# The clamp and the last subtraction of a float64 weight conversion, moved from VectorE to GpSimd

## The chip, the core and the metric

The kernel runs on one core of one Trainium2 chip. The core has TensorE (matmuls; PE in the profile, its weight loads PEld), VectorE (DVE), ScalarE (ACT) and GpSimd (POOL), and SyncE (SP), whose queue issues the DMAs of this kernel. The metric is the device time of one execution in microseconds (us); smaller is better.

## What is computed

Eight batches of an attention with a packed query, and then a feed-forward layer over all tokens:

```python
def sm_attn(qq, kk, vv):
    s = scale * np.matmul(qq, kk.transpose(0, 1, 3, 2))
    s = s - np.max(s, axis=-1, keepdims=True)
    a = np.exp(s)
    a = a / (np.sum(a, axis=-1, keepdims=True) + 1e-09)
    return np.matmul(a, vv)
p_packed = sm_attn(p, k, v)
out = sm_attn(q, p_packed, p_packed)
...
h = x @ w_in
g = np.maximum(h, 0.0) + alpha * np.minimum(h, 0.0)
return (g @ w_out).astype(np.float32)
```

There are 8 batches, 8 heads, 576 tokens, 64 columns per head and 32 packed queries; w_in is 512 x 2048 and w_out 2048 x 512. The activations are float32. The two weight matrices arrive as float64, and the kernel takes them as pairs of 32-bit words.

## The kernel before

Heads are taken in pairs (4 pairs, 128 partitions). `attention(b, tp)` does half a batch: it loads k, v and q, splits a float32 operand into a high part in the rounded format of the matmul and a low part that is the rest (`split_x`, L176; `split_v`, L306), and multiplies with both. The splits' low parts are GpSimd subtractions (L180, L311). For batches from 1 on, GpSimd also does the subtraction and the multiplication of the second softmax (L432, L439) and the low part of the result (L456). Batches 0 and 1 (`exact=True`) run on float32 without splits of q, k and v.

`packed_w` and its relatives multiply the packed values with w_in; `first(k, f)` gives one of 16 blocks f of the hidden layer for half a batch k (288 tokens), applies the leaky activation (L646 on ScalarE, L647 on VectorE) and splits the result (L652, L653); `second(k, f)` multiplies with block f of w_out and collects in four PSUM banks (L670 to L672).

**The conversion.** `convert` (L106) turns one tile of 128 x 512 float64 weights into float32. SP loads the raw words (L115). ScalarE takes the absolute value of the upper words, read as float32, into `mag` (L121), and the shifted lower words into `low` (L123). VectorE clamps `mag` to a range (L125), shifts its bits left by 3 and masks them (L128), puts sign and top bits from the raw tile in (L132), and adds `low` as an integer (L137 or L139). Where the whole float32 is wanted that is all (L137). Otherwise ScalarE rounds to the high part (L141), and VectorE subtracts it, which leaves the low part (L142). Every step reads what the step before it left in the same tile `mag`.

The conversion runs 32 times, every one with a clamp: 4 tiles of `packed_w_fine` and 4 of `packed_w_first` as whole float32; 8 tiles of `packed_w(..., "fresh")` and 16 of `convert_w_out` with high and low part, so that there are 24 subtractions. Eight more tiles of `packed_w(..., "whole")` are split by L573 and L574 without a conversion. The split w_in tiles are written to DRAM (L579) and read again by all later batches, so that conversions take place in the first quarter of the run only.

**What sets the order.** Each engine works through its own queue in order. The code is made of generators that the loop at L772 advances by a plan with start times (L759 to L769), around the sequence of `first` and `second`. This gives each instruction its place in the program; a planner with its own estimate of durations then fixes the order on each engine before the launch, and steps of several conversions and attentions are interleaved there much finer than the code reads. `mag` and `low` come from rings of three buffers (tags `xh` and `xl`, shared with `split_x`); the raw tiles from buffers that w_out tiles use later (`new_raw`, L144). A raw buffer can be loaded again when its last reader (L132) is through. All DMAs of the kernel stand in SP's single queue.

Of the kernel before, what the change touches and what calls it, by code (L numbers as in the profile page):

```python
# [13 lines left out]
ALU = mybir.AluOpType  # L14
# [8 lines left out]
def fv(ap):  # L23

    return ap.bitcast(F32)
# [3 lines left out]
def pack_attention_ffn_kernel(  # L29
# [20 lines left out]
    nc = tc.nc  # L50
# [24 lines left out]
    op = ctx.enter_context(tc.tile_pool(name="op", bufs=4))  # L75
# [30 lines left out]
    def convert(src, raw, place, whole=None, room=None):  # L106

        nc.sync.dma_start(out=raw if room is None else room, in_=src)  # L115
        yield
        u = raw.bitcast(U32).rearrange("p (f t) -> p f t", t=2)
        up = raw.bitcast(F32).rearrange("p (f t) -> p f t", t=2)[:, :, 1]
        mag = xin.tile([P, 512], F32, name="mag", tag="xh")
        bits = mag.bitcast(U32)  # L120
        nc.scalar.activation(out=mag, in_=up, func=AF.Abs)  # L121
        low = xin.tile([P, 512], U32, name="low", tag="xl")
        nc.scalar.activation(out=low, in_=u[:, :, 0], func=AF.Copy, scale=2.0**-29)  # L123
        yield
        nc.vector.tensor_scalar(  # L125
            out=mag, in0=mag, scalar1=F64_BOTTOM, scalar2=F64_TOP, op0=ALU.max, op1=ALU.min
        )
        nc.vector.tensor_scalar(  # L128
            out=bits, in0=bits, scalar1=3, scalar2=0x3FFFFFF8,
            op0=ALU.logical_shift_left, op1=ALU.bitwise_and,  # L130
        )
        nc.vector.scalar_tensor_tensor(  # L132
            out=bits, in0=u[:, :, 1], scalar=0xC0000000, in1=bits,
            op0=ALU.bitwise_and, op1=ALU.bitwise_or,
        )
        if whole is not None:
            nc.vector.tensor_tensor(out=whole().bitcast(U32), in0=bits, in1=low, op=ALU.add)  # L137
            return
        nc.vector.tensor_tensor(out=bits, in0=bits, in1=low, op=ALU.add)  # L139
        hi, lo = place()  # L140
        nc.scalar.copy(out=hi, in_=mag)  # L141
        nc.vector.tensor_tensor(out=lo, in0=mag, in1=fv(hi), op=ALU.subtract)  # L142

    def new_raw(f=0):  # L144

# [13 lines left out]
    def convert_w_out(f):  # L159
        def place():  # L160
            wo_t[f] = const.tile([P, 2, DM], F32R, name=f"wo{f}", tag=f"wo{f}")
            return wo_t[f][:, 0, :], wo_t[f][:, 1, :]

        return convert(w_out[f * P : (f + 1) * P, :], new_raw(f), place)
# [329 lines left out]
    def convert_w_in(j, pr, place, whole=None):  # L494
        src = w_in[pr * P : (pr + 1) * P, j * 512 : (j + 1) * 512]
        return convert(src, new_raw(), place, whole)

    def packed_w_fine(j):


        def get(f):
            cols = slice((4 * j + f) * P, (4 * j + f) * P + P)
            w = new_w32()
            raw = new_raw()
            steps = convert(
                w_in.rearrange("(r p) c -> p r c", p=P)[:, :, cols],
                raw, None, lambda: w, raw.rearrange("p (r c) -> p r c", r=NP),
            )
            drain(steps)
            nc.sync.dma_start(  # L510
                out=w_whole[j].rearrange("r p c -> p r c")[:, :, f * P : f * P + P],
                in_=w.rearrange("p (r c) -> p r c", r=NP),
            )
            return w
# [216 lines left out]
    def zipped(*gens):  # L731
# [11 lines left out]
        out=nal, in0=al, scalar1=-1.0, scalar2=1.0, op0=ALU.mult, op1=ALU.add  # L743
# [73 lines left out]
```

## Time and profile before

| | us |
|---|---|
| runs of the kernel before | 811.73, 815.4, 815.91 (median 815.4) |
| span of the profiled execution, first to last instruction | 809.3 |
| PE busy in the span | 773.0 |
| VectorE busy | 605.8 |
| ScalarE busy | 497.1 |
| GpSimd busy | 191.4 |
| clamps (L125) on VectorE, 32 | 13.3 |
| subtractions (L142) on VectorE, 16 + 8 | 10.9 + 5.7 |
| first and last clamp start | 13.0 and 202.1 |

The profile gives the span of its execution and no device time of its own beside it. The span leaves out what lies before the first and after the last instruction; the runs stand 2.4 to 6.6 us above it. Durations of VectorE instructions overlap by their pipeline, so that the distance of two starts is shorter than a duration. The rows of the profile have the form: line, engine, operation, output<-inputs, shapes, count, busy us and mean ns of one, idle time before it and what ended that. Timeline rows begin with start and length in us.

### The profile page before, as it was taken

How to read it: one execution, taken by the hardware profiler on the slowest of the kernel's cores; microseconds unless marked ns; L12 is line 12 of the kernel's file. 1: busy time of each engine (PE TensorE's matmuls, PEld its weight loads, DVE VectorE, ACT ScalarE, POOL GpSimd, SP SyncE). 2: the span in 40 equal slices, each digit the busy share in tenths (PEclk: the TensorE clock that was granted, in tenths of full speed). 3: DMA queues.
4: the chain of work that ended last, by engine and by line, in shares of the span. 5: the costliest groups of instructions: out<-in, count | busy, mean ns of one | idle time of the engine just before them, and what ended most of it. 6: DMA issues, size and time to landing. Idle time of an engine off the chain costs nothing.

```text
span 809.3 us, 14930 instructions
## 1 busy us (share of the span) xinstructions
PE 773.0 (96%) x5376; PEld 729.5 (90%) x5376; DVE 605.8 (75%) x1301; ACT 497.1 (61%) x1165; POOL 191.4 (24%) x195
## 2 busy tenths in 40 slices
PE   6779899999989899999999999999999999999997
PEld 4557688989989799999999999999999999999997
DVE  3998989877887656898896477987875566666664
ACT  4888798876767775665657756665567533333332
POOL 2101411235346212354342014534410000000000
PEclk9979999999999999999999999999999999999999
DMA  9976787422223843322216722311027000000000
GB/s 312 340 233 223 262 304 236 151 54 83 78 88 101 267 151 104 93 59 82 70 59 212 235 59 59 91 58 45 2 92 256 20 31 1 31 1 31 1 30 30
DMA packets 58457, 93.77 MB, mean 116 GB/s; under 512 B 5136, under 2 KB 36880, under 8 KB 58384
## 3 DMA queue, kind: packets, MB, share of 16 engines
q1 hardware_dynamic: 58384, 92.83, 35.7%
q8 instruction: 42, 0.69, 0.4%
q14 instruction: 31, 0.25, 0.1%
HBM read 72.88 MB, written 19.92 MB: 115 GB/s over the span
## 4 chain that ended last, share of the span: by engine, by line
PE 80%; DVE 8%; DMA 5%; ACT 5%; issue 1%; POOL 0%; SPq 0%; ACTq 0%; DVEq 0%
PE acc L670 15%; PE acc L671 15%; PE acc L672 15%; PE ps_h L640 7%; PE ps_h L641 7%; PE ps_h L642 7%; PE ps_h L628 3%; DMA vraw<-in_v 2%; PE ps_m L352 2%; PE ps_m L216 1%; PE ps_m L217 1%; PE ps_m L596 1%; PE ps_m L598 1%; PE ps_m L597 1%; DMA w<-w_split 1%
## 5 line engine op out<-in xcount | busy, mean ns | idle before, releaser
L670 PE MATMUL acc<-gh,wo 128*128 128x288 f32 x1024 | 286.2, 300 | 3.5 <-ACT gh L652 3.1
L671 PE MATMUL acc<-gh,wo 128*128 128x288 f32 x1024 | 281.8, 295 | 0.0
L670 PEld LDWEIGHTS acc<-gh,wo 128*128 128x128 f32 x1024 | 192.2, 188 | 9.8 <-ACT gh L652 5.6
L672 PE MATMUL acc<-gl,wo 128*128 128x288 f32 x1024 | 199.2, 299 | 0.0
L671 PEld LDWEIGHTS acc<-gh,wo 128*128 128x128 f32 x1024 | 192.4, 188 | 1.6 <-issue 0.2
L652 ACT CAST gh<-ps_h 128x288 fp32r<-128x288 f32 x256 | 101.6, 399 | 115.3 <-DVE ps_h L647 113.2
L646 ACT ACTIVATE neg<-ps_h 128x288 f32<-128x288 f32 x256 | 105.3, 412 | 107.2 <-PE ps_h L642 95.5
L653 DVE TENSOR_TENSOR gl<-ps_h,gh 128x288 fp32r<-128x288 f32 x256 | 115.2, 452 | 70.4 <-ACT gh L652 68.5
L647 DVE SCALAR_TENSOR_TENSOR ps_h<-neg,nal,ps_h 128x288 f32<-128x288 f32 x256 | 131.2, 515 | 47.2 <-ACT neg L646 46.5
L672 PEld LDWEIGHTS acc<-gl,wo 128*128 128x128 f32 x1024 | 157.4, 188 | 3.1 <-issue 0.4
L640 PE MATMUL ps_h<-a_h,pwh 128*128 128x288 f32 x448 | 134.2, 300 | 4.1 <-DVE gl L653 4.0
L641 PE MATMUL ps_h<-a_l,pwh 128*128 128x288 f32 x448 | 132.3, 295 | 0.0
L642 PE MATMUL ps_h<-a_h,pwl 128*128 128x288 f32 x448 | 132.1, 295 | 0.0
L180 POOL TENSOR_TENSOR xl<-xraw,xh 128x576 fp32r<-128x576 f32 x48 | 71.4, 1488 | 175.2 <-ACT xh L179 171.1
L616 DVE TENSOR_TENSOR pwl<-pw,pwh 128x512 fp32r<-128x512 f32 x112 | 83.7, 748 | 9.1 <-ACT pwh L613 3.5
L640 PEld LDWEIGHTS ps_h<-a_h,pwh 128*128 128x128 f32 x448 | 84.2, 188 | 6.1 <-DVE gl L653 5.3
L641 PEld LDWEIGHTS ps_h<-a_l,pwh 128*128 128x128 f32 x448 | 84.3, 188 | 0.6
L642 PEld LDWEIGHTS ps_h<-a_h,pwl 128*128 128x128 f32 x448 | 84.1, 188 | 0.2
L601 ACT COPY pw<-ps_m 64x512 f32<-64x512 f32 x120 | 69.6, 580 | 15.2 <-PE ps_m L598 12.5
L615 DVE CAST pwh<-pw 128x512 fp32r<-128x512 f32 x96 | 52.0, 542 | 28.6 <-PE ps_h L641 27.8
L311 POOL TENSOR_TENSOR vs<-vraw,vs 128x640 fp32r<-128x640 f32 x24 | 40.4, 1682 | 51.3 <-ACT vs L310 50.3
L628 PE MATMUL ps_h<-a_f,pw 128*128 128x288 f32 x128 | 39.6, 433 | 3.8 <-DVE a_f L444 3.0
(127 smaller groups left out, 991.4 us busy)
## 6 DMA issues: line engine op xcount, KB each, us to landing
w<-w_split SPq DMA_DIRECT2D x48, 512.0 KB, 4.2
xraw<-in_kT SPq DMA_DIRECT2D x32, 288.0 KB, 2.9
xraw<-in_qT SPq DMA_DIRECT2D x32, 288.0 KB, 2.9
outT<-ot SPq DMA_DIRECT2D x64, 144.0 KB, 2.2
vraw<-in_v SPq DMA_DIRECT2D x32, 256.0 KB, 2.9
wraw<-in_w_in SPq DMA_DIRECT2D x16, 512.0 KB, 5.6
wraw<-in_w_out SPq DMA_DIRECT2D x16, 512.0 KB, 4.9
w_split<-w SPq DMA_DIRECT2D x16, 512.0 KB, 4.2
```

Source lines behind the costliest of these rows:

```text
L180: nc.gpsimd.tensor_tensor(out=xl, in0=raw, in1=fv(xh), op=ALU.subtract)
L616: nc.vector.tensor_tensor(out=tl, in0=src, in1=fv(th), op=ALU.subtract)
L640: nc.tensor.matmul(ps[:, :HS], th[:, i, fs], a_h[:, i, tok], start=hi, stop=False)
L641: nc.tensor.matmul(ps[:, :HS], th[:, i, fs], a_l[:, i, tok], start=False, stop=False)
L642: nc.tensor.matmul(ps[:, :HS], tl[:, i, fs], a_h[:, i, tok], start=False, stop=lo)
L646: nc.scalar.activation(out=neg, in_=x, func=AF.Relu, scale=-1.0)
L647: nc.vector.scalar_tensor_tensor(out=x, in0=neg, scalar=nal[:, f : f + 1], in1=x, op0=ALU.mult, op1=ALU.add)
L652: nc.scalar.copy(out=gh, in_=x)
L653: nc.vector.tensor_tensor(out=gl, in0=x, in1=fv(gh), op=ALU.subtract)
L670: nc.tensor.matmul(acc[o][:, :HS], wo_t[f][:, 0, os_], gh, start=begin, stop=False)
L671: nc.tensor.matmul(acc[o][:, :HS], wo_t[f][:, 1, os_], gh, start=False, stop=False)
L672: nc.tensor.matmul(acc[o][:, :HS], wo_t[f][:, 0, os_], gl, start=False, stop=end)
```

## The change

The clamp (L125) and the last subtraction (L142) are issued to GpSimd; operands, operations, tiles and their place in the program stay.

```diff
         nc.scalar.activation(out=low, in_=u[:, :, 0], func=AF.Copy, scale=2.0**-29)
         yield
-        nc.vector.tensor_scalar(
+        nc.gpsimd.tensor_scalar(
             out=mag, in0=mag, scalar1=F64_BOTTOM, scalar2=F64_TOP, op0=ALU.max, op1=ALU.min
         )
...
         hi, lo = place()
         nc.scalar.copy(out=hi, in_=mag)
-        nc.vector.tensor_tensor(out=lo, in0=mag, in1=fv(hi), op=ALU.subtract)
+        nc.gpsimd.tensor_tensor(out=lo, in0=mag, in1=fv(hi), op=ALU.subtract)
```

## The prediction

> **What bounds it now.** I read the page first: its span, the forty slices and the chain that ended last.
>
> ```profile
> span 809.3 us, 14930 instructions
> DVE  3998989877887656898896477987875566666664
> POOL 2101411235346212354342014534410000000000
> PE 80%; DVE 8%; DMA 5%; ACT 5%; issue 1%; POOL 0%; SPq 0%; ACTq 0%; DVEq 0%
> ```
>
> A slice is 20.2 us. The chain is 80% PE, yet VectorE's digits are 8 and 9 in slices 2 to 7 while GpSimd's are 1 to 4. The conversions lie there, so I asked for busy times by stretch. The columns are the stretch, its length, then busy time and count for PE, PEld, DVE, ACT and POOL, the clock, DMA share and GB/s.
>
> ```profile
> 20.00:66.00 46.00, 36.15 (x179) 25.74 (x179) 44.15 (x96) 36.07 (x87) 5.64 (x12) 0.89 0.86 284
> 66.00:93.00 27.00, 25.20 (x134) 18.14 (x132) 23.86 (x47) 21.62 (x52) 7.36 (x8) 1.00 0.73 245
> 93.00:107.00 14.00, 13.55 (x74) 10.22 (x75) 12.29 (x23) 12.59 (x29) 3.27 (x4) 1.00 0.76 261
> 107.00:140.00 33.00, 30.64 (x192) 26.96 (x190) 31.60 (x65) 30.14 (x62) 5.20 (x3) 1.00 0.75 259
> 140.00:210.00 70.00, 68.22 (x463) 63.77 (x462) 56.31 (x133) 53.32 (x128) 25.14 (x25) 1.00 0.32 95
> ```
>
> From 20 to 140 us VectorE is busy 44.15 + 23.86 + 12.29 + 31.60 = 111.9 of 120 us, a share of 0.932, more than PE (105.5) or ScalarE (100.4); GpSimd has 21.5. After 140 us PE is busy 68.22 of 70, and what the other engines do there costs nothing as long as PE is fed. The start of the kernel is therefore the only place where the edit can tell, and a late start is not made good afterwards. The chain in order of time shows how VectorE sets the pace (start, length, what):
>
> ```profile
> 25.63 4.52 DMA wraw<-in_w_in
> ...
> 45.10 0.67 DVE t L439
> ...
> 45.87 0.78 ACT s_t L302
> ```
>
> Between the landing of the weights at 30.15 us and the softmax scaling at 45.87 nearly every piece of this chain is a VectorE one: attention waits behind conversions in VectorE's queue.
>
> **What is removed.** VectorE's groups between 20 and 140 us (busy us, mean ns, then idle before and its releaser):
>
> ```profile
> L132 DVE SCALAR_TENSOR_TENSOR mag<-wraw,mag 128x512 uint32<-128x512 uint32 x26 | 18.0, 691 | 0.1
> L139 DVE CUSTOM_DVE_ANT_0 mag<-mag,low 128x1024 uint16<-128x1024 uint16 x20 | 15.9, 802 | 0.1
> L125 DVE TENSOR_SCALAR mag<-mag 128x512 f32<-128x512 f32 x26 | 10.8, 418 | 2.8 <-ACT mag L121 2.8
> L128 DVE TENSOR_SCALAR mag<-mag 128x512 uint32<-128x512 uint32 x26 | 10.8, 418 | 0.1
> L142 DVE TENSOR_TENSOR wo<-mag,wo 128x512 fp32r<-128x512 f32 x12 | 8.2, 681 | 0.4 <-ACT wo L141 0.3
> L574 DVE TENSOR_TENSOR w<-w,w 128x512 fp32r<-128x512 f32 x8 | 6.4, 800 | 1.8 <-ACT w L573 1.7
> L142 DVE TENSOR_TENSOR w<-mag,w 128x512 fp32r<-128x512 f32 x8 | 5.7, 711 | 0.1
> L137 DVE CUSTOM_DVE_ANT_0 w<-mag,low 128x1024 uint16<-128x1024 uint16 x6 | 4.2, 692 | 0.0
> L616 DVE TENSOR_TENSOR pwl<-pw,pwh 128x512 fp32r<-128x512 f32 x5 | 3.3, 684 | 0.2 <-ACT pwh L613 0.2
> L432 DVE TENSOR_TENSOR t<-t,m 128x576 f32<-128x576 f32 x2 | 1.5, 763 | 0.0
> L439 DVE TENSOR_TENSOR t<-t,z 128x576 f32<-128x576 f32 x2 | 1.5, 746 | 0.0
> ```
>
> So 26 clamps (L125) and 12 + 8 = 20 subtractions (L142) leave VectorE in the stretch that counts; the few others stand before 20 us or behind 140 us, where they are covered by waits for DMA or by PE. Successive VectorE instructions overlap, so I count their pitch, from two pairs that ran back to back:
>
> ```profile
> 69.25 0.76 DVE L128 TENSOR_SCALAR mag<-mag 128x512 uint32<-128x512 uint32 x2
> 72.75 1.29 DVE L139 CUSTOM_DVE_ANT_0 mag<-mag,low 128x1024 uint16<-128x1024 uint16 x2
> ```
>
> The shift has the clamp's shape and mean (418 ns): 0.76 - 0.42 = 0.34 us. The addition has the subtraction's 128 x 512 words: 1.29 - 0.68 = 0.61, and I take 0.60. VectorE is relieved of 26 x 0.34 + 20 x 0.60 = 20.8 us.
>
> **What is added.** GpSimd ran neither operation, so its nearest rows set bounds. First its long groups between 20 and 140 us, then single instructions with little beside them, start and length first:
>
> ```profile
> L180 POOL TENSOR_TENSOR xl<-xraw,xh 128x576 fp32r<-128x576 f32 x2 | 3.6, 1792 | 24.2 <-ACT xh L179 24.2
> L456 POOL TENSOR_TENSOR a_l<-s,a_h 128x576 fp32r<-128x576 f32 x2 | 3.3, 1673 | 4.2 <-ACT a_h L455 4.2
> L432 POOL TENSOR_TENSOR t<-t,m 128x576 f32<-128x576 f32 x2 | 2.8, 1403 | 17.1 <-DMA w<-w_whole 11.7 <-DVE m L430 5.4
> ```
>
> ```profile
> 93.19 0.46 POOL L394 TENSOR_TENSOR pt<-ptf,pt 128x128 fp32r<-128x128 f32 x1
> 191.03 1.16 POOL L432 TENSOR_TENSOR t<-t,m 128x576 f32<-128x576 f32 x1 [0.20 <-DVE m L430]
> 204.99 1.42 POOL L180 TENSOR_TENSOR xl<-xraw,xh 128x576 fp32r<-128x576 f32 x1 [4.08 <-ACT xh L179]
> 1.35 0.53 POOL L100 MEMSET ptf<- 128x512 f32 x1
> ```
>
> The subtraction is L180's operation with 512 columns for 576. From 0.46 us at 128 columns to 1.42 at 576 each column costs 2.14 ns, so 512 take 1.28 us. Its ends are 1.03 (L432's 1.16 x 512/576) and 1.6 (L180's disturbed mean 1792 ns x 512/576). The clamp reads one tensor and does two operations: not under the 0.53 us of a memset that only writes 512 columns, not much over 1.03; I take 0.8, the middle. In the stretch GpSimd then gets 26 x 0.8 + 20 x 1.28 = 46.4 us on top of 21.5, 68 of 120: it has the room. Neither engine gets new DMAs to issue.
>
> But the two engines stand in each other's way. Two pairs show it:
>
> ```profile
> 84.90 1.40 POOL L439 TENSOR_TENSOR t<-t,z 128x576 f32<-128x576 f32 x1
> 85.20 1.65 DVE L139 CUSTOM_DVE_ANT_0 mag<-mag,low 128x1024 uint16<-128x1024 uint16 x1
> ```
>
> ```profile
> 90.72 1.70 POOL L456 TENSOR_TENSOR a_l<-s,a_h 128x576 fp32r<-128x576 f32 x1 [0.61 <-ACT a_h L455]
> 91.29 1.67 DVE L139 CUSTOM_DVE_ANT_0 mag<-mag,low 128x1024 uint16<-128x1024 uint16 x1
> ```
>
> GpSimd ends at 86.30 and 92.42, the additions at 86.85 and 92.96: each 0.55 us later, one undisturbed pitch. So the addition stood still until GpSimd was through and lost 1.0 us. GpSimd lost too: 1.70 us where 1.42 is undisturbed. That is a lock held for a whole instruction by VectorE operations with two inputs in SBUF.
>
> The Trainium skill says the same against this change (page "SBUF — State Buffer", section "Who interferes with whom"): VectorE's second port pair is GpSimd's only one, an exclusive lock, taken by a VectorE instruction with two SBUF inputs or in a two-port mode. The pairs above agree. It also counts a float32 tensor_scalar among the two-port ones; no row here isolates that.
>
> So I count the lock as a resource between 20 and 140 us. VectorE's kept users are L132, L139, L137, L574 and L616, 26 + 20 + 6 + 8 + 5 = 65 at 0.60 = 39.0; L432 and L439, 4 at 0.67 (their 0.75 less 0.08 of overlap) = 2.7; and L128, which runs at twice the others' rate and so is counted as one, 26 x 0.34 = 8.8: 50.5 us. With the 20.8 that leave and GpSimd's 21.5 that is 92.8 of 120 us now. Afterwards it is 50.5 + 21.5 + 46.4 = 118.4. The change frees an engine that was full and fills the lock that this engine shares. No engine in this stretch reaches more than 0.932 of it; at that share 118.4 us need 127.0, which is **7.0 us** more. On the profile's span that makes 816.3; the median of the runs stands 6.1 us over the span (815.4 to 809.3), so **822** in their terms.
>
> Two waits lie inside this sum. L128 follows the clamp in VectorE's queue and waits for GpSimd; behind it stand the PSUM operations that feed PE (L647, L653). And SP's queue already waits for conversions (total us, times, longest):
>
> ```profile
> SPq L115 <- DVE mag L132: 19.6, 15, 3.2
> SPq L579 <- DVE w L142: 9.7, 4, 3.7
> ```
>
> A raw buffer is free only after L132, so a late clamp also delays the next weight load and every load behind it; the w_split write will wait for GpSimd instead of L142. A new hand-over, by the 2.8 us that L125 waited over 26 times for ScalarE, costs 0.11 us, 2.8 in all; this counts only where the lock does not already.
>
> **Rivals.** First, the relief reaches the end: **faster**. If the clamp is at its low end, 0.53, and the subtraction at 1.03, GpSimd gets 34.4 us and the lock 106.4, no longer the bound. VectorE then keeps 111.9 - 20.8 = 91.1, plus 2.8 for hand-overs, plus blocking. The two pairs shown cost 2.0 us for 3.1 us of GpSimd, but GpSimd's other long instructions met operations on PSUM; I set a third of its added time, 11.5. That is 105.4 / 0.932 = 113.1, 6.9 us less: 808.5. PE's own 105.5 us bounds it. For it: VectorE's share is largest just where chain pieces are its own. Against it: GpSimd's rows in this stretch are already its slow ones (1673 and 1792 ns against 1420).
>
> By the Trainium skill ("GPSIMD Engine Reference", "Elementwise — side-by-side cycle accounting" and "Engine selection") a two-input operation takes 1.96 times VectorE's and a one-input one about line rate; as an estimate 1.2 us and, at 512 columns by 1.2 GHz, 0.43 us. The sum by them is 50.5 + 21.5 + 35.2 = 107 us, close to this rival. No run here shows either price yet.
>
> Second, **no change**: L128 does not take the lock. Then the lock needs 109.6, at 0.932 117.6 us, 2.4 less: 813. The same outcome comes if GpSimd's instructions fall beside VectorE's reductions and PSUM work half of the time: blocking of 23.2 us against a relief of 20.8, 2.4 more: 818. For it: of GpSimd's long instructions only some show a blocked partner.
>
> Third, GpSimd is **much slower** at both: clamp 1.03, subtraction 1.6. Added 58.8, lock 130.8, 140.3 us at that share: 20 us more, 835. It decides if the mean clamp is over about 1 us.
>
> The order on the engines is also made anew by the planner; chance alone may bring 3 or 4 us of either sign, which lies inside each case.
>
> **How the numbers follow.** Slower as forecast 0.40, much slower 0.10, no change 0.26, faster 0.24. The measurement tells about 0.5% (4 us) from nothing. The range reaches from the faster rival, 807 with a little for order, to 834, just short of the third rival: what is left out on both sides is about 2 in 10. The slower cases' own range is 818 to 836. Faster by over 0.5%: 0.24; within: 0.26; slower: 0.50.
>
> **What would show it.** In the changed profile L125 on POOL should be near 0.8 us and L142 near 1.3, longer where VectorE works; the means of L132, L139 and L574 should rise over 0.69, 0.80 and 0.80; waits of L128 for the clamp should appear; and the time at which PE's busy share reaches 98% should come later than 140 us. The forecast is wrong if those means stay, if VectorE's share between 20 and 140 falls below 0.85, or if the start is shorter.

## The result, and the profile after

The changed kernel takes 834.11 us (median of 4 runs, 832.77 to 835.24) against 814.07 for the kernel before in the same series: 1.0243 times as long, 95% interval 1.0208 to 1.0277, 20 us slower. The forecast was slower, 822, with a range from 807 to 834. The profiles show one execution each, that of 832.77 us for the changed kernel, so that their spans differ by 21.7 us and the medians by 20.0.

The page of the changed kernel, the lines that answer to those of before:

```profile
span 831.0 us, 14962 instructions
DVE  3898769767777746788897567888886466666663
POOL 3888657634564401343643113344221000000000
PE 76%; DVE 8%; ACT 3%; DMA 3%; issue 2%; POOL 2%; ACTq 0%; SPq 0%; DVEq 0%; POOLq 0%
```

GpSimd's digits rise in the first ten slices: they were 0 to 5 and are 3 to 8. VectorE's fall only a little. The same stretches as in the prediction (stretch, length, then PE, PEld, DVE, ACT and POOL busy, clock, DMA share, GB/s):

```profile
20.00:66.00 46.00, 34.51 (x180) 25.77 (x180) 42.07 (x72) 35.16 (x83) 38.94 (x29) 0.89 0.83 270
66.00:93.00 27.00, 24.72 (x130) 17.22 (x128) 22.37 (x38) 19.03 (x46) 19.75 (x16) 1.00 0.64 195
93.00:107.00 14.00, 11.78 (x49) 7.43 (x50) 10.10 (x16) 11.26 (x27) 8.45 (x10) 0.88 0.84 266
107.00:140.00 33.00, 28.81 (x172) 24.18 (x171) 28.07 (x50) 26.02 (x52) 22.08 (x14) 1.00 0.65 224
140.00:210.00 70.00, 65.83 (x442) 61.85 (x441) 50.52 (x107) 52.73 (x124) 36.64 (x28) 0.98 0.38 123
```

From 20 to 140 us VectorE is busy 102.6 us instead of 111.9, GpSimd 89.2 instead of 21.5, and PE only 99.8 instead of 105.5. The two moved groups on GpSimd and the users of the port on VectorE, between 20 and 140 us:

```profile
L125 POOL TENSOR_SCALAR mag<-mag 128x512 f32<-128x512 f32 x25 | 51.4, 2064 | 7.8 <-ACT mag L121 5.8 <-DMA wraw<-in_w_in 2.0
L142 POOL TENSOR_TENSOR wo<-mag,wo 128x512 fp32r<-128x512 f32 x12 | 16.4, 1363 | 1.4 <-ACT wo L141 1.1
...
L132 DVE SCALAR_TENSOR_TENSOR mag<-wraw,mag 128x512 uint32<-128x512 uint32 x26 | 20.9, 805 | 0.4
L128 DVE TENSOR_SCALAR mag<-mag 128x512 uint32<-128x512 uint32 x25 | 19.0, 761 | 2.5 <-POOL mag L125 2.4
L139 DVE CUSTOM_DVE_ANT_0 mag<-mag,low 128x1024 uint16<-128x1024 uint16 x18 | 17.1, 952 | 0.2
```

The clamp's mean is 2064 ns where the prediction took 800. L128's mean goes from 418 to 761 ns, L132's from 691 to 805, L139's from 802 to 952: VectorE's busy time falls by 9.3 us and not by the 20.8 that the prediction took off it, mainly because the instructions that it kept are longer. All 32 clamps, and the subtractions into wo (shortest, median and longest ns):

```profile
L125 POOL TENSOR_SCALAR mag<-mag x32: 1908/1918/2459, 13.2 to 221.3; 128x512 f32<-128x512 f32 x32
```

```profile
L142 POOL TENSOR_TENSOR wo<-mag,wo x16: 1257/1294/1719, 29.1 to 228.1; 128x512 fp32r<-128x512 f32 x16
```

How late PE is can be read from its matmul records, 5376 in both kernels. First before, then after:

```profile
20.00:140.00 120.00, 105.54 (x575) 81.06 (x574) 111.90 (x228) 100.42 (x226) 21.46 (x26) 0.96 0.79 265
140.00:230.00 90.00, 86.83 (x592) 81.40 (x590) 73.40 (x170) 66.49 (x159) 36.18 (x34) 1.00 0.34 104
230.00:809.30 579.30, 568.48 (x4167) 557.76 (x4167) 412.72 (x882) 321.09 (x758) 129.43 (x117) 1.00 0.26 80
```

```profile
20.00:140.00 120.00, 99.82 (x526) 74.61 (x526) 102.61 (x173) 91.48 (x206) 89.22 (x66) 0.94 0.74 240
140.00:230.00 90.00, 81.12 (x527) 74.95 (x526) 65.73 (x142) 65.26 (x155) 47.88 (x38) 0.97 0.34 109
230.00:831.00 601.00, 585.43 (x4287) 574.00 (x4286) 430.35 (x913) 333.98 (x784) 138.01 (x126) 1.00 0.26 82
```

Behind 230 us a microsecond holds 4167 / 579.3 = 7.2 records. At 230 us the changed kernel has 4287 - 4167 = 120 more of them to do, 16.7 us; the last 5 us of the 21.7 come later. Of the 120 records, 592 - 527 = 65 were lost between 140 and 230, 55 earlier. Before 140 us records are longer (575 in 120 us, 4.8 in a microsecond), so that those 55 stand for some 11 us and not for 55 / 7.2 = 7.6. The same matmul in both traces says this directly: the 85th of L670 starts at 141.30 us in the kernel before and 11.5 us later in the changed one, the 169th (206.21 us before) 9.7 us later, the 211th (238.33 us before) 17.0 us later. So about half of the loss falls where the prediction looked for all of it, and the next 7 us come between 206 and 238.

One gap between 140 and 230 shows how the late part comes about. First GpSimd, then the chain of waits behind it (start, length, what):

```profile
223.84 1.85 POOL L180 TENSOR_TENSOR xl<-xraw,xh 128x576 fp32r<-128x576 f32 x1 [0.64 <-ACT xh L179]
```

```profile
224.79 1.45 DVE mag L132
226.24 0.06 DVE den L299
226.30 0.43 DVE ps_h L647
226.73 0.59 DVE mag L139
227.33 0.09 DVE den L300
227.41 0.00 issue
227.42 0.63 ACT wo L141
228.04 0.06 issue
228.10 0.45 PE ps_m L330
```

The last conversion of the kernel now starts its clamp at 221.3 us instead of 202.1. Its L132 stands still until GpSimd's L180 is through at 225.69; behind it in the same queue stand its L139 and the softmax's small instructions (L299, L300). The trace has PE idle for 3.2 us before the transpose L330. The chain names ScalarE's rounding (L141) as the last piece, because it ended last; but L330 reads s_t, whose last writer ran beside it, behind L300 on VectorE:

```profile
227.44 0.52 DVE L304 TENSOR_SCALAR s_t<-s_t,den 128x576 f32<-128x576 f32 x1
```

### The profile page after: what moved, and what is told of

It is laid out like the page before. It is cut to its first block, busy times and chain, and to the rows that moved or that the text cites. A ratio compares the mean times of both kernels' runs of the same rounds, so it can differ in the third digit from the quotient of the medians.

```text
span 831.0 us, 14962 instructions
## 1 busy us (share of the span) xinstructions
PE 777.4 (94%) x5376; PEld 732.2 (88%) x5376; DVE 604.6 (73%) x1245; ACT 499.5 (60%) x1165; POOL 283.3 (34%) x251
## 4 chain that ended last, share of the span: by engine, by line
PE 76%; DVE 8%; ACT 3%; DMA 3%; issue 2%; POOL 2%; ACTq 0%; SPq 0%; DVEq 0%; POOLq 0%
PE acc L670 15%; PE acc L671 15%; PE acc L672 14%; PE ps_h L640 7%; PE ps_h L641 7%; PE ps_h L642 6%; PE ps_h L628 2%; PE ps_m L216 1%; PE ps_m L217 1%; PE ps_m L352 1%; PE ps_m L596 1%; PE ps_m L598 1%; PE ps_m L597 1%; DVE pwl L616 1%; DVE mag L132 1%
## 5 line engine op out<-in xcount | busy, mean ns | idle before, releaser
L670 PE MATMUL acc<-gh,wo 128*128 128x288 f32 x1024 | 288.4, 301 | 12.1 <-ACT gh L652 10.1
L670 PEld LDWEIGHTS acc<-gh,wo 128*128 128x128 f32 x1024 | 193.2, 189 | 21.0 <-ACT gh L652 14.4
L672 PE MATMUL acc<-gl,wo 128*128 128x288 f32 x1024 | 203.2, 299 | 0.0
L672 PEld LDWEIGHTS acc<-gl,wo 128*128 128x128 f32 x1024 | 159.4, 189 | 2.5
L180 POOL TENSOR_TENSOR xl<-xraw,xh 128x576 fp32r<-128x576 f32 x48 | 69.9, 1458 | 137.5 <-ACT xh L179 132.0
L616 DVE TENSOR_TENSOR pwl<-pw,pwh 128x512 fp32r<-128x512 f32 x112 | 88.2, 789 | 12.5 <-ACT pwh L613 3.5
L125 POOL TENSOR_SCALAR mag<-mag 128x512 f32<-128x512 f32 x32 | 64.9, 2034 | 26.8 <-ACT mag L121 24.8
L311 POOL TENSOR_TENSOR vs<-vraw,vs 128x640 fp32r<-128x640 f32 x24 | 38.5, 1603 | 47.9 <-ACT vs L310 45.7
```

What stands on the lines that cost most here:

```text
L180: nc.gpsimd.tensor_tensor(out=xl, in0=raw, in1=fv(xh), op=ALU.subtract)
L616: nc.vector.tensor_tensor(out=tl, in0=src, in1=fv(th), op=ALU.subtract)
L670: nc.tensor.matmul(acc[o][:, :HS], wo_t[f][:, 0, os_], gh, start=begin, stop=False)
L672: nc.tensor.matmul(acc[o][:, :HS], wo_t[f][:, 0, os_], gl, start=False, stop=end)
```

## The experiments

Two theories stood at first. **A, the port**: GpSimd's reads keep VectorE's instructions standing. **B, the length**: the clamp is long and stands in the chain of every conversion. A third came up on the way, **the order**: any edit makes the planner order all queues anew. The differences below are ratios to the kernel before in the same series, times about 815 us.

### One half at a time

e1 moves the clamp alone, e2 the subtraction alone:

```diff
-        nc.vector.tensor_scalar(            # e1: this line alone
+        nc.gpsimd.tensor_scalar(
...
-        nc.vector.tensor_tensor(out=lo, in0=mag, in1=fv(hi), op=ALU.subtract)   # e2: this line alone
+        nc.gpsimd.tensor_tensor(out=lo, in0=mag, in1=fv(hi), op=ALU.subtract)
```

> Only the clamp goes to GpSimd; the subtraction stays on VectorE. Theory A (port): the subtractions that GpSimd reads through the shared port keep VectorE standing; without them the loss falls to 5 us or less over the kernel before. Theory B (length): the clamp takes 1.92 us on GpSimd where VectorE's pitch was 0.34, and this stands in the chain of every conversion and in GpSimd's queue; the loss stays at 13 to 20 us.

> Only the subtraction goes to GpSimd; the clamp stays on VectorE. Theory A: the loss stays at 10 us or more over the kernel before. Theory B: within 4 us of the kernel before, on either side, because the subtraction is the last step of a conversion and VectorE is relieved of 0.60 us for each.

Measured: e1 822.33 us, 1.0089 (1.0055 to 1.0124), 7 us; e2 825.61 us, 1.0118 (1.0083 to 1.0153), 10 us. Neither theory alone fits both: the clamp costs more than A allows and less than B says, the subtraction about what A says. Both halves cost, and together (17 us) a little less than the whole (20).

### The clamp made shorter

e3 clamps 64 columns of 512, e4 drops the upper bound:

```diff
-            out=mag, in0=mag, scalar1=F64_BOTTOM, scalar2=F64_TOP, op0=ALU.max, op1=ALU.min
+            out=mag[:, :64], in0=mag[:, :64], scalar1=F64_BOTTOM, scalar2=F64_TOP, op0=ALU.max, op1=ALU.min   # e3
+            out=mag, in0=mag, scalar1=F64_BOTTOM, scalar2=None, op0=ALU.max   # e4
```

> Both on GpSimd as in the changed kernel, but the clamp works on the first 64 of 512 columns only, so the other 448 columns stay unclamped; hand-overs between the engines stay as they are. Clamp about 0.4 us instead of 1.92. Theory A: still 10 us or more slower than the kernel before. Theory B: within 5 us of the kernel before.

> Both on GpSimd, the clamp with its lower bound only (one operation for each element instead of two; the upper bound is left out). This prices the second operation: between 1.0 and 1.9 us a clamp. Theory A: time unchanged within 4 us of the changed kernel. Theory B: the loss of about 20 us shrinks in proportion to what the clamp loses, some 10 us back if the clamp takes 1.1 us.

Measured: e3 824.56 us, 1.0105 (1.0075 to 1.0136); e4 829.9 us, 1.018 (1.0145 to 1.0215). The clamps' rows, e3 and then e4:

```profile
L125 POOL TENSOR_SCALAR mag<-mag x32: 417/448/971, 12.9 to 212.2; 128x64 f32<-128x64 f32 x32
```

```profile
L125 POOL TENSOR_SCALAR mag<-mag x32: 1478/1494/2027, 12.7 to 217.8; 128x512 f32<-128x512 f32 x32
```

With the clamp at 0.45 us the kernel costs as much as with the subtraction alone (e2), so hand-overs by themselves look cheap; at 9 us it fits neither A (10 or more) nor B (5 or less). With one operation the clamp takes 1.49 instead of 1.92 us, and 5 us come back. This looked like B for the clamp; but each of these kernels has an order of its own.

### Idle work on GpSimd

e5 is a control that only changes the order. e6 to e8 leave VectorE's work alone and give GpSimd idle work for each conversion, in a small tile that nobody reads:

```diff
+        low = xin.tile([P, 512], U32, name="low", tag="xl")          # e5: low before mag
+        nc.scalar.activation(out=low, in_=u[:, :, 0], func=AF.Copy, scale=2.0**-29)
         nc.scalar.activation(out=mag, in_=up, func=AF.Abs)
-        low = xin.tile([P, 512], U32, name="low", tag="xl")
-        nc.scalar.activation(out=low, in_=u[:, :, 0], func=AF.Copy, scale=2.0**-29)
...
+        dump = xin.tile([P, 128], F32, name="dump", tag="dump", bufs=1)
+        for i in range(4):                                           # e6; e7: the clamp's tensor_scalar
+            q = fv(low)[:, i * 128 : i * 128 + 128]
+            nc.gpsimd.tensor_tensor(out=dump, in0=q, in1=q, op=ALU.subtract)
...
+        nc.gpsimd.tensor_copy(out=dump[:, 0:1], in_=fv(low)[:, 0:1])  # e8
+        for _ in range(11):
+            nc.gpsimd.memset(dump, 0.0)
```

> The kernel before with ScalarE's two reads of a raw tile issued in the other order (the low words first), no work moved. The planner gives PE a new order in some 570 lines, about as many as with the clamp alone on GpSimd. This sizes what a new order alone does: every theory expects no more than 4 us either way; if it is 7 us or more, the loss of the single halves (7 and 9 us) can be order and nothing else.

> The kernel before, unchanged on VectorE, with four idle subtractions of 128 columns added on GpSimd for each of the 32 conversions, about 1.8 us together, that read a finished tile and write one nobody reads. Theory A (port): VectorE's instructions with two inputs in SBUF grow and the kernel loses 6 us or more. Theory B (length of the conversion's chain): no chain is longer, so within 3 us of the kernel before.

> The same with four idle clamps of 128 columns for each conversion, about 2 to 2.6 us together. If a clamp holds the port as a subtraction does, the loss is like that of the idle subtractions or larger; if it holds it little, as the changed kernel's trace looks (two-input instructions of VectorE run on beside clamps), 0 to 4 us. Theory B: within 3 us.

> The same with memsets on GpSimd that read nothing, about 2 us for each conversion. GpSimd's queue is as full as with the idle clamps, but nothing is read from SBUF. Theory A: within 2 us of the kernel before, VectorE's durations unchanged. If a full GpSimd queue by itself delays attention's GpSimd steps, 4 us or more slower.

Measured: e5 817.26 us, 1.0025 (1.0004 to 1.0047); e6 823.27, 1.0125 (1.0084 to 1.0166); e7 825.28, 1.0127 (1.0082 to 1.0172); e8 820.18, 1.0063 (1.0031 to 1.0094). e5 stayed within the 4 us that were expected. e6 is as A says, 10 us with no chain longer, but in a new order. e7, in a new order too, cost as much, against the expectation; its four pieces took 0.78 us each, 3.1 us a conversion, and filled GpSimd to 97.9 of 120 us. e8 was expected to cost nothing and cost 5 us, in exactly the order of the kernel before on PE, VectorE, ScalarE and SP. VectorE's clamp (line 129 there) is longer:

```profile
L129 DVE TENSOR_SCALAR mag<-mag 128x512 f32<-128x512 f32 x26 | 12.4, 480 | 3.4 <-ACT mag L121 3.3
```

The mean is 480 ns instead of 418, but it holds some collisions with reading instructions; the 21 clamps of the whole run that had memsets alone beside them took 446 ns on average and at most 532, the 5 with nothing beside them 428. This explains little of the 5 us: the VectorE instructions that begin before 230 us in the kernel before, matched one by one since the order is the same, took only 0.9 us longer in all. Two other causes stay open. GpSimd is busy for 93.4 of the 120 us, and attention's steps stand in its queue; and ScalarE waits 5.1 us, in 5 times, until the idle copy has released a buffer of `low`.

### Work taken away, and a longer ring

e9 leaves the clamp out; e10 also puts a memset on GpSimd in the place of the subtraction; e11 and e12 give the ring of mag a fourth buffer, in the changed kernel and in the kernel before:

```diff
-        nc.vector.tensor_scalar(            # e9, e10
-            out=mag, in0=mag, scalar1=F64_BOTTOM, scalar2=F64_TOP, op0=ALU.max, op1=ALU.min
-        )
...
-        nc.vector.tensor_tensor(out=lo, in0=mag, in1=fv(hi), op=ALU.subtract)   # e10
+        nc.gpsimd.memset(fv(lo), 0.0)
...
-        mag = xin.tile([P, 512], F32, name="mag", tag="xh")                     # e11, e12; xh too
+        mag = xin.tile([P, 512], F32, name="mag", tag="xh", bufs=4)
-    op = ctx.enter_context(tc.tile_pool(name="op", bufs=4))
+    op = ctx.enter_context(tc.tile_pool(name="op", bufs=2))
```

> The kernel before without the clamp on any engine (tiny and huge weights are not bounded). VectorE is relieved of 26 x 0.34 = 8.8 us between 20 and 140 us and nobody pays. If VectorE's full queue sets the pace there, as the prediction read it, 5 us or more faster; if only a few waits of the stretch hang on it, within 3 us of the kernel before.

> No clamp, and the subtraction replaced by a memset of the low part on GpSimd (the low parts of the 24 split tiles are zero). VectorE is relieved of all 20.8 us in the stretch, GpSimd gets only 20 short writes. If VectorE sets the pace: 10 to 18 us faster, so that the change gave away as much again as it lost. If it does not: within 5 us.

> The changed kernel with four buffers instead of three in the ring of mag and xh (and two instead of four for the output tiles, which pays for the space). If the longer stay of a tile in the ring holds conversions up (theory B), 6 us or more come back against the changed kernel; if port and queue do it (theory A), 0 to 3 us.

> The control: the kernel before with the same rings. All theories: within 4 us of the kernel before. The gain of the fourth buffer in the changed kernel is read against this one.

Measured: e9 820.46 us, 1.0072 (1.0044 to 1.0099); e10 821.08, 1.0082 (1.0058 to 1.0105); e11 838.48, 1.0282 (1.0245 to 1.032); e12 831.58, 1.0207 (1.017 to 1.0244). Taking work from the fullest engine made the kernel **slower**, and so did the longer ring; all four expectations failed here, that of the control e12 by most (17 us instead of at most 4). Read against this control, as was planned, the fourth buffer leaves the changed kernel 7 us behind instead of 20, which is what B expected of it; but e12 has another order and fewer output buffers as well, so that this is not shown. e10's stretch from 20 to 140 us:

```profile
20.00:140.00 120.00, 102.17 (x549) 78.73 (x550) 90.96 (x182) 101.34 (x227) 26.29 (x43) 0.94 0.82 283
```

VectorE has 91.0 us left of 111.9, all the relief that was to be had, and PE still does 549 records instead of 575. Its longest wait is for the result of batch 0's attention (L441 is L444 of the kernel before; total, times, longest):

```profile
PE ps_h L625 <- DVE a_f L441: 8.5, 2, 7.0
```

In the kernel before PE's one wait for this tile took 3.0 us. Since e10's VectorE has less to do and GpSimd got only short writes, the order of the queues is the likely cause; it was not isolated. The same goes for e12: it differs from the kernel before in buffers, and in the order that the planner made with them.

### The same order, and the same change from other orders

f1 and f2 are e6 and e7 with three and two pieces, issued ahead of the generator's next step, with which the planner gives PE, VectorE, ScalarE and SP exactly the order of the kernel before. f3 has a multiplication by 1 on GpSimd for the clamp, and every queue exactly as in the changed kernel. f4 is the change made on e5; f5 and f6 are the kernels before and after under the planner's plainer rule:

```diff
+            for i in range(3):      # f1: tensor_tensor as in e6; f2: range(2), tensor_scalar as in e7
...
-            out=mag, in0=mag, scalar1=F64_BOTTOM, scalar2=F64_TOP, op0=ALU.max, op1=ALU.min
+            out=mag, in0=mag, scalar1=1.0, scalar2=None, op0=ALU.mult      # f3
...
-    with tile.TileContext(nc, schedule_with_timeline_sim=True) as tc:
+    with tile.TileContext(nc, schedule_with_timeline_sim=False) as tc:     # f5, f6
```

> The kernel before with three idle subtractions of 128 columns on GpSimd for each conversion (about 1.6 us together), chosen so that the order on PE, VectorE, ScalarE and SP is that of the kernel before, instruction for instruction. Port theory: VectorE's two-input instructions grow and 5 us or more are lost with no new order. Order theory: within 2.5 us of the kernel before.

> The same with two idle clamps of 128 columns for each conversion (about 1.6 us together), again with the order of the kernel before. Port theory with a clamp that holds the port little: 2 to 5 us, about what the memsets cost (5 us). If a clamp holds the port as a subtraction does: as f1. Order theory: within 2.5 us.

> The changed kernel with a multiplication by 1 in place of the clamp on GpSimd (the weights are not bounded), one operation per element; the order on all engines is exactly that of the changed kernel. If the clamp's length counts (about 7 us for each microsecond, from clamps of 0.61, 1.65 and 2.06 us so far), a multiplication of 1.1 to 1.6 us gives back 3 to 6 us. If the order alone made the loss: nothing comes back, within 2 us of the changed kernel.

> The whole change made from e5 (ScalarE's two reads in the other order), which stood 0.25% over the kernel before. If the loss belongs to the change: again 15 to 25 us over e5, a ratio of 1.02 to 1.033 to the kernel before. If the one order of the kernel before was lucky: 8 us or less over e5, at most 1.0125.

> The kernel before, with the planner's detailed timing switched off, so that it orders the queues by its plainer rule; no work is changed. A kernel whose start is tuned to one order loses here: 5 us or more over the kernel before (as e12 did with 17). If order matters little: within 4 us.

> The changed kernel under the same plainer rule. If the loss belongs to the change: 10 us or more over f5. If it is mostly the departure from one good order: 8 us or less over f5, or even faster than f5.

Measured: f1 819.62 us, 1.0048 (1.0025 to 1.0071), 4 us; f2 816.4, 1.0005 (0.9977 to 1.0034), nothing. GpSimd's idle groups between 20 and 140 us, f1 and then f2, and VectorE's subtraction into wo in each (681 ns in the kernel before):

```profile
L111 POOL TENSOR_TENSOR dump<-low 128x128 f32<-128x128 f32 x79 | 48.0, 608 | 36.6 <-ACT low L123 30.7 <-ACT c L357 1.3
L142 DVE TENSOR_TENSOR wo<-mag,wo 128x512 fp32r<-128x512 f32 x12 | 9.6, 797 | 0.1
```

```profile
L111 POOL TENSOR_SCALAR dump<-low 128x128 f32<-128x128 f32 x53 | 42.3, 799 | 40.2 <-ACT low L123 36.0 <-ACT c L357 1.7
L142 DVE TENSOR_TENSOR wo<-mag,wo 128x512 fp32r<-128x512 f32 x12 | 8.5, 711 | 0.0
```

With 48 and 42 us of GpSimd time in the same stretch, the idle subtractions lengthen VectorE's subtraction from 681 to 797 ns, the idle clamps to 711. L128 took 552 ns on average where it had idle subtractions alone beside it (16 times) and 465 beside idle clamps alone (17 times), against 419 with nothing beside it. Over all VectorE instructions up to 230 us, matched as for e8, f1 is 8.2 us longer and f2 4.0. So the port is real for subtractions, without any new order, and small (4 us of time); clamps lengthen VectorE's instructions by less, and in the time they do not show.

f3 took 836.41 us, 1.0238 (1.018 to 1.0297), though its instruction is as short as e4's (median 1500 ns): 0.4 us less for each of 32 and nothing back in the median, though with four runs and an interval of about 5 us either way. The 5 us of e4, whose order is another, were therefore not shown to be the clamp's length. f4 took 832.91 us, 1.0203 (1.0159 to 1.0247); f5 854.62, 1.048 (1.0431 to 1.0529); f6 888.44, 1.0892 (1.0845 to 1.094). The same change, from four orders of the kernel before (e5 and f4 stand in different series; by their ratios they differ by 14.5 us):

| kernel before | changed | difference of the medians |
|---|---|---|
| as given, 814.07 | 834.11 | 20.0 us |
| e5, 817.26 | f4, 832.91 | 15.7 us |
| e12, 831.58 | e11, 838.48 | 6.9 us |
| f5, 854.62 | f6, 888.44 | 33.8 us |

In f6 VectorE waits for the clamp itself (between 20 and 300 us; total, times, longest):

```profile
DVE mag L128 <- POOL mag L125: 22.4, 15, 3.6
```

That is 1.5 us a time. In the changed kernel the same wait between 20 and 300 us was 3.2 us in 4 times: how much of the clamp's length is waited for depends on the order.

**The granted clock.** Every run also has TensorE's mean granted clock. In the 63 runs of the kernel before in these series it lies between 0.982 and 0.994, and a straight line through them falls by 6.0 us for each 0.01. The changed kernel's runs have 0.980 to 0.984 and lie 15.9 us over that line, f3 14.8. At equal clock, by the same line (extended a little below its range), f4 lies 11 us over e5, e11 7 over e12, f6 26 over f5; f1 stands 3.6 us over the line, f2 1.3, e9 and e10 3.7 and 3.6. The signs stay, the sizes move by some microseconds. Whether a lower clock makes part of the loss, or follows from PE's gaps, is not shown.

**What stays open.** The change costs time from each of four orders, which speaks against the order alone, though each changed kernel has an order of its own too; its size, 7 to 34 us, depends on the order, so it is not the port alone either. How the 20 us divide is not settled: no run has the changed kernel's order with the work on the old engines. One path was not tried by itself: up to 140 us SP's queue waited 19.6 us for L132 in the kernel before, 28.2 in e1, 27.7 in e2 and 37.6 in the changed kernel, so that weight loads waited longer with each part of the change.

## Why the prediction was right or wrong

**The sign was right; the main terms behind it were not.** The steps that failed are the clamp's price, 0.8 us where 1.92 was measured, and the count of the lock, in which every GpSimd instruction held it to its end. The loss was 20 us and not 7. The runs show some 4 us for the lock of subtractions by itself (f1); how the rest divides between the clamp's length, the new order and later weight loads stays open.

- **The clamp's price was mis-sized.** "Not under the 0.53 us of a memset that only writes 512 columns, not much over 1.03; I take 0.8": measured 1.92 us undisturbed, 26 x 1.92 = 49.9 us instead of 20.8. The upper bound came from a two-input operation, on the thought that one input is cheaper; here it was dearer. The third rival named the condition, a clamp over 1 us, with a chance of 0.10. That its 835 us lies next to the measured 834 is luck: it had the clamp at 1.03 and the subtraction at 1.6, both wrong, and the same count of the lock.
- **The subtraction's price held**: 1.28 us forecast, median 1.29.
- **The lock held for subtractions, and for clamps only in small part.** The subtraction's collisions came as described. This is GpSimd, then VectorE, in the changed kernel:

```profile
123.19 1.28 POOL L142 TENSOR_TENSOR w<-mag,w 128x512 fp32r<-128x512 f32 x1
```

```profile
123.25 1.50 DVE L128 TENSOR_SCALAR mag<-mag 128x512 uint32<-128x512 uint32 x1 [1.58 <-POOL mag L125]
```

  L128 ends at 124.75, 0.28 us behind the subtraction, so L128 is a user of the port as counted, and the second rival's first condition falls. But three clamps in a row let two-input instructions pass:

```profile
32.92 6.13 POOL L125 TENSOR_SCALAR mag<-mag 128x512 f32<-128x512 f32 x3
```

```profile
33.94 0.64 DVE L137 CUSTOM_DVE_ANT_0 w<-mag,low 128x1024 uint16<-128x1024 uint16 x1
34.51 0.73 DVE L439 TENSOR_TENSOR t<-t,z 128x576 f32<-128x576 f32 x1
```

  Both ran in their undisturbed time beside a clamp. Others did not; beside the third of these clamps, which ends at 39.05:

```profile
37.16 0.86 DVE L128 TENSOR_SCALAR mag<-mag 128x512 uint32<-128x512 uint32 x1
```

  That is 0.44 us more than undisturbed. Of the 37 L128, L132 and L139 with clamps alone beside them, four L128 lost 0.41 to 0.44 us, and three L132 and three L139 lost 0.30; none of these ten stood until the clamp's end. With the true price the prediction's own sum would be 50.5 + 21.5 + 49.9 + 25.6 = 147.5 us, 158 at the share of 0.932, a loss of 38: too much, since it counts clamps as holders to their end. Too short a clamp and too strict a lock partly cancelled. The Trainium skill's exclusive lock (page "SBUF — State Buffer", section "Who interferes with whom") agrees with the subtraction; that the loser stands for the whole instruction does not hold for these clamps, and here the trace decides.
- **"After 140 us PE is busy, and what the other engines do there costs nothing" was wrong for the changed kernel.** By the matmuls of L670 it is 11.5 us late at 141 us and 17.0 us late at 238, as the conversions moved later.
- **That a full VectorE sets the pace was not borne out.** e9 and e10 free 8.8 and 20.8 us of it and are 6 to 7 us slower, both in a new order. A busy share of 0.932 and a chain of VectorE pieces were not enough to make its time the kernel's time. With this the division by 0.932 and the first rival's gain lose their ground.
- **The order was mis-sized**: "3 or 4 us of either sign". Five kernels with the same work or less were 2, 6, 7, 17 and 39 us slower (e5, e9, e10, e12, f5), none faster.
- Of the signs named, the longer means of L132 and L139 and the waits of L128 came, and PE's full share came later; L574's mean fell from 800 to 746 ns where it was to rise. VectorE's share, 102.6 of 120 or 0.855, stayed just above the limit named, 0.85. The waits of SP's queue for L132 grew as foreseen, from 19.6 to 37.6 us up to 140 us.
- Two readings of the prediction are off, without touching its 7.0 us. GpSimd's digits in slices 2 to 7 are 0 to 4, not 1 to 4. And its 6.1 us from span to run compare one execution's span with the median of others: in the changed kernel's traced execution, span and run are 1.8 us apart (831.0 and 832.77).

## What to carry to other kernels

Price a moved operation by the same kind of instruction on the new engine, not by one that looks simpler: where no row has it, the bound must stay open to the slow side. Before a busy engine's work is moved, take the work away altogether and see whether the kernel gets faster; if it does not, there is little for the move to win. Where a planner orders the queues, this test too comes with a new order: add a control that changes the order alone, and look for loads that leave the order as it is.

## What the runs showed of the hardware

GpSimd's tensor_scalar on 128x512 float32 took 1.92 us with two operations (max, min), 1.49 with one (max) and 1.50 with a multiplication; on 64 columns 0.45. The two-input subtraction of the same shape took 1.29. So the operation that reads less took longer, and most of VectorE's two-input instructions ran on beside it; those that were held up lost 0.3 us and not the clamp's whole length. GpSimd memsets, which read nothing, lengthened VectorE's clamp a little: 446 ns on average, at most 532, with memsets alone beside it, against 428 with nothing beside it in the same run.
